# Agent attention with a gated convolution: a batch's transposed rows in one buffer of five pairs, and loads that the planner holds back

## The chip, the core and the metric

The kernel runs on one core of one Trainium2 chip. The metric is device time in microseconds (us): the median of several runs of the same program. Beside it stands one profiled execution, whose trace shows each instruction of each engine: TensorE (PE, with its weight loads as PEld), VectorE (DVE), ScalarE (ACT), GpSimd (POOL) and SyncE (SP), whose queue (SPq) issues nearly all the DMAs.

## What is computed

Four batches of 12,800 rows with 128 columns, 49 agents. Attention runs twice, from agents to keys and from queries to agents; its output goes through a causal convolution of five taps that gates a projection.

```python
def sm(a, b):                       # softmax over the last axis
    s = scale * (a @ b.transpose(0, 2, 1))
    e = np.exp(s - s.max(-1, keepdims=True))
    return e / (e.sum(-1, keepdims=True) + 1e-09)

agent_v = sm(agents, k) @ v                      # 49 x 128 per batch
x = sm(q, agents) @ agent_v                      # 12800 x 128 per batch

xp = zeros for 4 rows, then x                    # the convolution looks back
gate_pre = sum over k in 0..4 of conv_w[k] * xp[:, k:k + S, :]
out = (sigmoid(gate_pre) * (x @ w_val)) @ w_out
```

## The kernel before

**Units, pairs and chunks.** A batch is cut into ten units of 1,280 rows; two units form a pair (`SEG` = 2,560 rows), five pairs a batch. The output is made in chunks of 512 rows, five per pair, 100 in all (the last one is cut in two).

**Stages.** For each unit of keys (`k`, line 392) PE makes scores against the agents, ACT copies them, DVE takes their maximum. For each unit of values (`v`, `agent_values`, line 461) ACT takes the exponentials, DVE transposes them, PE accumulates the agents' values in `av`. `fold` (line 513) then folds agents' values, convolution weights and `w_val` of the batch into stationary matrices `stat`, so that x itself is never made: chunks work on the attention weights of the queries. For each unit of queries (`q`, line 733) PE makes scores, DVE, POOL and ACT turn them into softmax weights, and POOL and ACT write them as half-precision pieces to `pt` (lines 778 to 798): the weights, their remainders and some copies, 128 columns for each row.

**Transposed rows.** `transposes` (`t`, line 827) turns `pt` into rows along the free axis of `x1`: the first four units through PE, the other 36 by a DMA transpose that SyncE issues (line 835, `x<-pt`). `x1s` is a ring of four buffers (line 221), each with `PAD` = 16 columns ahead of one pair. `shifts` (line 866) makes `x2` from `x1`: two DMAs (line 884, `x<-x`) copy some rows five times, each time shifted by one column, for a matmul that does five taps at once. From the fifth unit on there is one such couple of DMAs per pair, once both transposes of the pair have landed.

**The preceding columns.** The convolution looks back four rows. The first four columns that a pair needs lie at the end of the pair before, in another buffer. `halo` (line 813) has POOL copy these four columns in front of the pair (line 819), or set them to zero where a batch begins (line 816).

**Chunks.** `gates` (`g`, line 898): five matmuls on `x1`, each one column further (line 922), and one on `x2` (line 926); ACT takes the tanh. `values` (`a`, line 942): two matmuls (lines 949 and 953); DVE multiplies (line 962), ACT rounds to half precision (line 968), POOL takes the remainder `hl` (line 973). `project` (`o`, line 979): three matmuls (lines 992 to 994), ACT scales (line 1006), SyncE stores each two chunks (line 1021).

**Loads.** Each unit of k, q or v is one load of 640 or 645 KB (line 369) into a ring of `NLOAD` = 11 buffers `ld`; 120 units in all. There is no load for a batch after the last, so from the last `v` on only the loads of q are left.

**What sets the order.** The order of PE's work is written out as a string (`order`, line 1088, for instance `q2.4 k3.0 g47 a47 o45`: queries of batch 2, unit 4, then keys of batch 3, unit 0, then chunk 47). For all other engines, the `Plan` (line 68) makes a schedule: every step has an engine, an estimated duration, and the steps that it needs; DMAs also have a time on the wire. `order()` (line 94) goes through the steps in time. Of those ready on an engine it takes the one with the longest path behind it (`tail`). A load is ready as soon as the last reader of its buffer is done. The result is sorted by planned start and issued in that order, so each engine's queue, SyncE's among them, is fixed beforehand; on the chip an instruction at the head of its queue waits for what it needs, and all behind it wait too. The planner's figures set only this order, not the time.

Of the kernel before, what the change touches and what calls it, by code (L numbers as in the profile page):

```python
# [10 lines left out]
F16 = mybir.dt.float16  # L11
# [6 lines left out]
P = 128  # L18
# [4 lines left out]
UNIT = 1280  # L23
NBLK = 10
GT = UNIT // G
SEG = 2 * UNIT
CH = 512
TAPS = 5
HALO = TAPS - 1
PAD = 16  # L30
# [8 lines left out]
NLOAD = 11  # L39
NT_, NH = 3, 3  # L40
NPT = 4
NX = 4
CUT = 2
NOB = 4
LEAD = 5
# [13 lines left out]
BACKLOG = 3.0  # L59
LANES = 8  # L60
LAND = 1.4

QS = 256.0
WS = 64.0
# [3 lines left out]
class Plan:  # L68
# [22 lines left out]
        self.steps.append((engine, us, fn, need, moved, key))  # L91
        self.urge.append(urge)

    def order(self):
        n = len(self.steps)
        after = [[] for _ in range(n)]
        last = None
        for i, (engine, us, fn, need, moved, key) in enumerate(self.steps):
            for j in need:
                after[j].append(i)  # L100
            if engine == "pe":
                if last is not None and last not in need:
                    after[last].append(i)
                last = i
        tail = [0.0] * n
        for i in reversed(range(n)):
            engine, us, fn, need, moved, key = self.steps[i]
            cost = us + HOP + (moved + LAND if moved else 0.0)
            if engine == "pe":
                cost = us  # L110
            tail[i] = cost + self.urge[i] + max((tail[j] for j in after[i]), default=0.0)
        engines = ("pe", "act", "dve", "pool", "dma")
        free = dict.fromkeys(engines, 0.0)
        wire = 0.0
        lanes = [0.0] * LANES
        left = [len(s[3]) for s in self.steps]
        at = [0.0] * n
        queues = {e: [] for e in engines}
        pe = [i for i, s in enumerate(self.steps) if s[0] == "pe"]
        here = 0  # L120
        for i, s in enumerate(self.steps):
            if s[0] != "pe" and not left[i]:
                queues[s[0]].append(i)
        start = [0.0] * n
        kind = None
        done = 0
        while done < n:
            best = None
            free["dma"] = max(free["dma"], wire - BACKLOG, lanes[0])
            for e in engines:  # L130
                if e == "pe":
                    if here < len(pe) and not left[pe[here]]:
                        pick, when = pe[here], max(free[e], at[pe[here]])
                    else:
                        continue
                elif queues[e]:
                    q = queues[e]
                    soon = min(max(free[e], at[i]) for i in q)
                    open_ = [i for i in q if at[i] <= soon + 0.05]
                    pick = max(open_, key=lambda i: (tail[i], -i))  # L140
                    for i in q:
                        if tail[i] > tail[pick] + 1.0 and at[i] < soon + 0.6 * self.steps[pick][1]:
                            pick = i
                    when = max(free[e], at[pick])
                else:
                    continue
                if best is None or when < best[0]:
                    best = when, e, pick
            when, e, i = best
            engine, us, fn, need, moved, key = self.steps[i]  # L150
            if e == "pe":
                here += 1
                if key != kind:
                    when += 0.12
                kind = key
            else:
                queues[e].remove(i)
            start[i] = when
            free[e] = when + us
            end = when + us + HOP  # L160
            if moved:
                wire = max(wire, when + 0.5) + moved
                end = max(wire, when + us) + LAND
                lanes = lanes[1:] + [end]
            done += 1
            for j in after[i]:
                if i in self.steps[j][3]:
                    left[j] -= 1
                    at[j] = max(at[j], end)
                    if not left[j] and self.steps[j][0] != "pe":  # L170
                        queues[self.steps[j][0]].append(j)
        self.start = start
        return sorted(range(n), key=lambda i: (start[i], i))


@with_exitstack
def tile_agent_attention_gated_conv(
# [9 lines left out]
    nc = tc.nc  # L187
# [30 lines left out]
    qsm = ring(2, [P, NBLK], F32, "qsm")  # L218
    qr = ring(2, [P, NBLK], F32, "qr")
    pts = ring(NPT, [P, NBLK, P], F16, "pt")  # L220
    x1s = ring(NX, [P, PAD + SEG], F16, "x1_")
    x2s = ring(3, [P, SEG], F16, "x2")
    ths = ring(NT_, [P, CH], F32, "th")
    hs = ring(NH, [P, CH], F32, "h")
# [41 lines left out]
        out=fold, in0=ident[:, 0:AP_], in1=ident[:, AP_:P], op=ALU.add  # L266
    )
    nc.vector.memset(tiny, 1e-9 / QS)
    nc.vector.memset(x1s[0][:, 0:PAD], 0.0)
    for t in wst_sb:  # L270
        nc.gpsimd.memset(t[:, TAPS + 1 :, :], 0.0)

# [81 lines left out]
    def load(kind, b, u):  # L354
        i = taken[0] % NLOAD
        taken[0] += 1
        slot_of[kind, b, u] = i
        if kind == "v":
            dst, src = ld[i], vP[b, u].rearrange("p n c -> p (n c)")
        else:  # L360
            dst = ld[i][:, 0:UNIT]
            src = (kT if kind == "k" else qT)[b, :, u * UNIT : (u + 1) * UNIT]
        parts = [(dst, src, [("ld", i), ("ld2", i)])]
        if (kind, b, u) == ("v", 0, NU - 1):
            h = VW // 2
            parts = [(dst[:, 0:h], src[:, 0:h], [("ld", i)]), (dst[:, h:], src[:, h:], [("ld2", i)])]
        for d, f, keys in parts:
            add(
                "dma", 0.4, lambda d=d, f=f: nc.sync.dma_start(out=d, in_=f), (), keys,
                1.57 / len(parts),  # L370
            )

    def score_matmuls(b, src, out):
# [425 lines left out]
    def on_pe(b, u):  # L799
        g = b * NU + u  # L800
        return g < PE_FIRST or (g < (B - 1) * NU and g % TURN in PE_TURNS)

    def unit_rows(g):
        o = PAD + g % 2 * UNIT
        return x1s[g // 2 % NX][:, o : o + UNIT]

    def row_keys(s, halves):


        i = s % NX  # L810
        return [(x, i, h) for h in halves for x in ("x1", "x1b")] + [("x1h", i)] * (0 in halves)

    def halo(s):
        to = x1s[s % NX][:, PAD - HALO : PAD]
        if s * 2 % NU == 0:
            fn = lambda: nc.gpsimd.memset(to, 0.0)
            read = []
        else:
            fn = lambda: nc.gpsimd.tensor_copy(
                out=to, in_=x1s[(s - 1) % NX][:, PAD + SEG - HALO : PAD + SEG]  # L820
            )
            read = [(x, (s - 1) % NX, 1) for x in ("x1", "x1b")]

        read.append(("x2", (s - 1) % 3, UNIT, 0))
        add("pool", 0.1, fn, read, [("x1h", s % NX)])

    def transposes(b, u):
        g = b * NU + u
# [37 lines left out]
    def shifts(b, u):  # L866

        g = b * NU + u
        if g >= SINGLE and g % 2 == 0:
            return  # L870
        n = 1 if g < SINGLE else 2
        u0 = u + 1 - n
        s = g // 2
        x2, x1 = x2s[s % 3], x1s[s % NX]
        o = (g + 1 - n) % 2 * UNIT
        src = row_keys(s, range(0, g % 2 + 1))
        c = PAD - HALO + o
        for r0, r1, every, us in X2CUTS:
            first = A + (2 if every == 3 else 3 * THREES)
            rows = x1[first : first + 1 + (r1 - r0 - 1) * every : every, c : c + 1]  # L880
            view = [rows.ap[0], (1, TAPS), (1, n * UNIT)]
            add(
                "dma", 0.6,
                lambda r0=r0, r1=r1, rows=rows, view=view: nc.sync.dma_start(
                    out=x2[r0 * TAPS : r1 * TAPS, o : o + n * UNIT],
                    in_=bass.AP(rows.tensor, rows.offset, view),
                ),
                src, [("x2", s % 3, o + i * UNIT, r0) for i in range(n)], us * n,
            )
        if g % 2 and (g + 1) // 2 < B * NU // 2:  # L890
            halo((g + 1) // 2)


    chunks = [(t // NCH, t % NCH * CH, CH) for t in range(NT - 1)]
# [3 lines left out]
    def gates(t):  # L898
# [10 lines left out]
        halves = sorted({(b * NU + n // UNIT) % 2 * UNIT for n in (n0, n0 + w - 1)})  # L909
        segs_ = sorted({(b * NU + n // UNIT) // 2 for n in (n0, n0 + w - 1)})  # L910
        assert len(segs_) == 1
        x2, x1 = x2s[segs_[0] % 3], x1s[segs_[0] % NX]
        o2 = n0 - (segs_[0] * SEG - b * N)
        xs = row_keys(segs_[0], halves_)
        x2k = [("x2", segs_[0] % 3, h, c[0]) for h in halves for c in X2CUTS]
# [2 lines left out]

        def matmuls():
            for k in range(TAPS):  # L920
                c = PAD - HALO + o2 + k
                nc.tensor.matmul(  # L922
                    out=pg, lhsT=stat[:, k, :], rhs=x1[:, c : c + w],
                    start=(k == 0), stop=False,
                )
# [9 lines left out]
            lambda: nc.scalar.activation(out=th, in_=pg, func=AF.Tanh, scale=unscale[:, 0:1]),  # L935
            [at_g, ("unscale", x)], [("th", t % NT_)],
        )
        return stat, x2, o2, xs, x2k, st, th

    state = {}  # L940

    def values(t):
        b, n0, w = chunks[t]
        stat, x2, o2, xs, x2k, st, th = state.pop(t)
        pv, at_v = banks[t][2:]
        scale = w / CH

        def matmuls():
            nc.tensor.matmul(  # L949
                out=pv, lhsT=stat[:, TAPS, :], rhs=x1s[(b * NCH + n0 // CH) // 5 % NX][:, PAD + o2 : PAD + o2 + w],  # L950
                start=True, stop=False,
            )
            nc.tensor.matmul(  # L953
# [184 lines left out]
            done += 1  # L1138
        run[w[0]](*w[1:])

    for i in plan.order():
        plan.steps[i][2]()


# [42 lines left out]
```

## Time and profile before

| | us |
|---|---|
| median of 3 runs | 425.89 (425.65 to 426.75) |
| span of the profiled execution | 423.6 |
| PE busy | 403.9 |
| ACT busy | 301.5 |
| DVE busy | 293.3 |
| POOL busy | 228.2 |

The rows of the profile read thus. A row of a timeline has start and length in us, engine, line of the kernel, operation, tiles written and read (buffer numbers left out), and a count where several instructions are merged; in square brackets the idle time ahead of it and what ended it. `SPq` rows are DMAs being issued: their length is how long SyncE was at it, not how long the data took. In the chain of waits, `DMA x<-pt` with a length is the stretch from issue to landing. The DMA row of the page shows the busy share of the core's sixteen DMA engines in tenths, in 40 equal slices of the span.

### The profile page before, as it was taken

The page shows a single profiled execution, that of the slowest core. Times are in us where ns is not written, and L with a number is a line of the kernel's source. Part 1 is how long each engine was busy: PE and PEld are TensorE (multiplying, and loading weights), DVE is VectorE, ACT ScalarE, POOL GpSimd, SP SyncE. Part 2 cuts the span into 40 slices and gives each one's busy share as a digit, 9 for nine tenths or more (in the row PEclk, how much of TensorE's full clock was granted, in tenths as well). Part 3 has the DMA queues.
Part 4 walks back from the last instruction along what each step waited for, and adds up shares of the span by engine and source line. Part 5 has one row for each costly group of instructions (what it writes and reads, how often), then busy time and mean ns, then how long its engine had stood idle before and what let it go on. Part 6 is the DMA issues. An engine that isn't in the chain of part 4 may idle for free.

```text
span 423.6 us, 10042 instructions
## 1 busy us (share of the span) xinstructions
PE 403.9 (95%) x3907; PEld 197.0 (47%) x3907; DVE 293.3 (69%) x562; ACT 301.5 (71%) x521; POOL 228.2 (54%) x263
## 2 busy tenths in 40 slices
PE   4979999999999999999999899999999989999995
PEld 1358434346555443446555343335555534344443
DVE  3757899867875978667795575767765678676231
ACT  1564568779966777678876486778876567788776
POOL 1002557654657565554566355574366277877553
PEclk9969999999999999999999899999999999999998
DMA  8999999999999999999999999999999977755733
GB/s 320 420 417 411 370 367 353 301 295 310 412 293 283 346 317 362 304 278 356 351 379 324 271 299 370 314 332 302 296 393 322 239 196 161 199 163 176 205 121 124
DMA packets 75129, 127.62 MB, mean 301 GB/s; under 512 B 50466, under 2 KB 50850, under 8 KB 75084
## 3 DMA queue, kind: packets, MB, share of 16 engines
q1 hardware_dynamic: 74940, 126.87, 96.9%
q8 instruction: 30, 0.49, 0.5%
q10 hardware_dynamic: 144, 0.13, 0.2%
q14 instruction: 15, 0.12, 0.1%
HBM read 79.25 MB, written 26.21 MB: 249 GB/s over the span
## 4 chain that ended last, share of the span: by engine, by line
PE 78%; DMA 9%; DVE 8%; ACT 1%; POOL 1%; issue 1%; SPq 0%; POOLq 0%; DVEq 0%; ACTq 0%
PE gate L922 23%; PE sc L376 17%; PE av L480 10%; PE val L949 5%; PE out L992 5%; PE val L953 5%; PE gate L926 5%; PE out L993 4%; DMA ld<-kT 4%; PE out L994 4%; DMA x<-pt 3%; DMA x<-x 2%; DVE h L962 1%; DVE qw L772 1%; DVE qsm L763 1%
## 5 line engine op out<-in xcount | busy, mean ns | idle before, releaser
L973 POOL TENSOR_TENSOR hl<-h,hh 128x512 f16<-128x512 f32 (+1 forms) x101 | 116.9, 1158 | 96.1 <-ACT hh L968 96.0
L922 PE MATMUL gate<-x,stat 128*128 128x512 f16 (+1 forms) x500 | 125.2, 380 | 0.2 <-ACT th L935 0.2
L962 DVE SCALAR_TENSOR_TENSOR h<-th,val 128x512 f32<-128x512 f32 x100 | 67.8, 678 | 66.8 <-PE out L993 26.2
L376 PE MATMUL sc<-ld,ag_sb 128*32 128x320 f32 x1280 | 101.5, 447 | 7.6 <-DMA ld<-kT 7.0
L935 ACT ACTIVATE th<-gate,unscale 128x512 f32<-128x512 f32 x100 | 68.3, 683 | 33.3 <-PE gate L926 31.7
L1006 ACT ACTIVATE ob<-out,oscale 128x512 f32<-128x512 f32 x98 | 67.3, 687 | 21.3 <-PE out L994 20.1
L922 PEld LDWEIGHTS <-stat 128*128 128x128 f16 x505 | 46.3, 97 | 63.7 <-issue 14.8
L968 ACT CAST hh<-h 128x512 f16<-128x512 f32 (+1 forms) x101 | 61.5, 609 | 17.2 <-DVE h L962 16.4
L750 POOL TENSOR_TENSOR qw<-sT,qmx 128x490 f32<-128x490 f32 x40 | 41.4, 1035 | 47.6 <-DVE qmx L745 47.5
L376 PEld LDWEIGHTS sc<-ld,ag_sb 128*32 128x32 f32 x1280 | 36.7, 111 | 59.4 <-issue 25.7
L480 PE MATMUL av<-ld,eT 128*32 128x129 f32 (+1 forms) x1400 | 50.7, 279 | 1.0 <-DVE eT L386 1.0
L480 PEld LDWEIGHTS av<-ld,eT 128*32 128x32 f32 (+1 forms) x1400 | 47.1, 117 | 7.5 <-issue 2.5
L794 POOL TENSOR_TENSOR pt<-qw,pt 128x490 f16<-128x490 f32 x40 | 44.8, 1120 | 3.1 <-ACT pt L779 2.9
L471 ACT ACTIVATE e<-ks,kbias 128x320 f32<-128x320 f32 x80 | 39.3, 554 | 5.4 <-DVE eT L386 3.3
L386 DVE STREAM_TRANSPOSE sT<-sc 128x640 f32<-128x640 f32 x40 | 33.6, 839 | 13.4 <-PE sc L376 12.7
L402 ACT COPY ks<-sc 128x640 f32<-128x640 f32 x40 | 27.7, 691 | 21.2 <-PE sc L376 19.1
L386 DVE STREAM_TRANSPOSE eT<-e 128x640 f32<-128x640 f32 x40 | 33.5, 842 | 9.8 <-ACT e L471 5.2
L926 PE MATMUL gate<-x,stat 95*128 95x512 f16 x100 | 38.3, 383 | 1.5 <-DMA x<-x 1.5
L949 PE MATMUL val<-x,stat 128*128 128x512 f16 x100 | 38.2, 382 | 0.8 <-DVE h L962 0.6
L953 PE MATMUL val<-x,stat 95*128 95x512 f16 x100 | 38.1, 381 | 0.0
L994 PE MATMUL out<-hl,wo 128*128 128x512 f16 x98 | 37.0, 378 | 1.1 <-POOL hl L973 1.1
L992 PE MATMUL out<-hh,wo 128*128 128x512 f16 x98 | 37.3, 381 | 0.1
(130 smaller groups left out, 389.4 us busy)
## 6 DMA issues: line engine op xcount, KB each, us to landing
ld<-kT SPq DMA_DIRECT2D x40, 640.0 KB
ld<-qT SPq DMA_DIRECT2D x40, 640.0 KB
ld<-vP SPq DMA_DIRECT2D x39, 645.0 KB
outT<-ob SPq DMA_DIRECT2D x48, 512.0 KB
x<-x SPq DMA_DIRECT2D x18, 375.0 KB
x<-x SPq DMA_DIRECT2D x18, 100.0 KB
outT<-ob SPq DMA_DIRECT2D x3, 256.0 KB
x<-x SPq DMA_DIRECT2D x4, 187.5 KB
```

Of the source, the lines that this page charges most:

```text
L376: nc.tensor.matmul(out=out[g * BLK : (g + 1) * BLK, j, 0:GT], lhsT=ag_sb[:, b, j * BLK : (j + 1) * BLK], rhs=src[:, g * GT : (g + 1) * GT] ...
L386: nc.vector.transpose(out=out.rearrange("p n (j i) -> p j n i", j=2), in_=in_.rearrange("p j (n i) -> p j n i", i=BLK),)
L480: nc.tensor.matmul(out=av[o + j : o + j + cols, 0 : C + 1], lhsT=et[:, n, j : j + cols], rhs=vt[:, n, :], start=(u == 0 and n < 2), stop=( ...
L922: nc.tensor.matmul(out=pg, lhsT=stat[:, k, :], rhs=x1[:, c : c + w], start=(k == 0), stop=False,)
L926: nc.tensor.matmul(out=pg, lhsT=stat[0 : TAPS * X2R, TAPS + 1, :], rhs=x2[0 : TAPS * X2R, o2 : o2 + w], start=False, stop=True,)
L935: lambda: nc.scalar.activation(out=th, in_=pg, func=AF.Tanh, scale=unscale[:, 0:1]),
L949: nc.tensor.matmul(out=pv, lhsT=stat[:, TAPS, :], rhs=x1s[(b * NCH + n0 // CH) // 5 % NX][:, PAD + o2 : PAD + o2 + w], start=True, stop=False,
L953: nc.tensor.matmul(out=pv, lhsT=stat[0 : TAPS * X2R, TAPS + 2, :], rhs=x2[0 : TAPS * X2R, o2 : o2 + w], start=False, stop=True,)
L962: lambda: nc.vector.scalar_tensor_tensor(out=h, in0=th, scalar=1.0, in1=pv, op0=ALU.add, op1=ALU.mult),
L968: "act", 0.16 + 0.42 * scale, lambda: nc.scalar.copy(out=hh, in_=h),
L973: lambda: nc.gpsimd.tensor_tensor(out=hl, in0=h, in1=hh, op=ALU.subtract),
L1006: lambda: nc.scalar.activation(out=ob[:, o : o + w], in_=po, func=AF.Copy, scale=oscale),
```

## The change

There are two parts.

One: `x1` is one buffer of `NX` = 5 pairs behind 16 zero columns. A pair's place is its number modulo five, so the first pair of each batch always comes behind the zero columns, and every other pair right behind the pair before. `halo` and its 19 POOL instructions are gone. `row_keys` makes a reader of a pair's first half also a reader of the second half of the pair before (in the planner's bookkeeping). Shifts and matmuls take their columns from the one buffer; their shapes stay.

Two: `late_loads` takes the place of `order` at the end. It makes the plan once as before, notes for each load the planned start of the first step that reads it, and makes the plan again with each load not ready earlier than `AHEAD` = 14 us before that start. PE's written order stays.

```diff
-NX = 4
+NX = 5
...
+AHEAD = 14.0
...
-    def order(self):
+    def order(self, held=None):
...
-        at = [0.0] * n
+        at = list(held or [0.0] * n)
...
+    def late_loads(self):
+        self.order()
+        held = [0.0] * len(self.steps)
+        for i, s in enumerate(self.steps):
+            for j in s[3]:
+                if self.steps[j][5] == "ld":
+                    t = self.start[i] - AHEAD
+                    held[j] = min(held[j], t) if held[j] else t
+        return self.order(held)
...
-    x1s = ring(NX, [P, PAD + SEG], F16, "x1_")
+    x1 = const.tile([P, PAD + NX * SEG], F16, name="x1")
...
-    nc.vector.memset(x1s[0][:, 0:PAD], 0.0)
+    nc.vector.memset(x1[:, 0:PAD], 0.0)
...
-                1.57 / len(parts),
+                1.57 / len(parts), key="ld",
...
+    def pair_at(s):
+        return PAD + s % NX * SEG
+
     def unit_rows(g):
-        o = PAD + g % 2 * UNIT
-        return x1s[g // 2 % NX][:, o : o + UNIT]
+        o = pair_at(g // 2) + g % 2 * UNIT
+        return x1[:, o : o + UNIT]
 
     def row_keys(s, halves):
-        i = s % NX
-        return [(x, i, h) for h in halves for x in ("x1", "x1b")] + [("x1h", i)] * (0 in halves)
-
-    def halo(s):
-        to = x1s[s % NX][:, PAD - HALO : PAD]
-        if s * 2 % NU == 0:
-            fn = lambda: nc.gpsimd.memset(to, 0.0)
-            read = []
-        else:
-            fn = lambda: nc.gpsimd.tensor_copy(
-                out=to, in_=x1s[(s - 1) % NX][:, PAD + SEG - HALO : PAD + SEG]
-            )
-            read = [(x, (s - 1) % NX, 1) for x in ("x1", "x1b")]
-
-        read.append(("x2", (s - 1) % 3, UNIT, 0))
-        add("pool", 0.1, fn, read, [("x1h", s % NX)])
+        keys = [(x, s % NX, h) for h in halves for x in ("x1", "x1b")]
+        if 0 in halves and s % NX:
+            keys += [(x, s % NX - 1, 1) for x in ("x1", "x1b")]
+        return keys
...
-        c = PAD - HALO + o
+        c = pair_at(s) - HALO + o
...
-        if g % 2 and (g + 1) // 2 < B * NU // 2:
-            halo((g + 1) // 2)
...
-                c = PAD - HALO + o2 + k
+                c = o1 - HALO + o2 + k
...
-    for i in plan.order():
+    for i in plan.late_loads():
         plan.steps[i][2]()
```

More of the change, by code (lines that the diff above doesn't have):

```diff
@@ L873, in shifts @@
         s = g // 2
-        x2, x1 = x2s[s % 3], x1s[s % NX]
+        x2 = x2s[s % 3]
         o = (g + 1 - n) % 2 * UNIT
         src = row_keys(s, range(0, g % 2 + 1))
-        c = PAD - HALO + o
+        c = pair_at(s) - HALO + o
         for r0, r1, every, us in X2CUTS:
@@ L911, in gates @@
         assert len(segs_) == 1
-        x2, x1 = x2s[segs_[0] % 3], x1s[segs_[0] % NX]
+        x2 = x2s[segs_[0] % 3]
+        o1 = pair_at(segs_[0])
         o2 = n0 - (segs_[0] * SEG - b * N)
@@ L937, in gates @@
         )
-        return stat, x2, o2, xs, x2k, st, th
+        return stat, x2, o1 + o2, o2, xs, x2k, st, th
     state = {}
@@ L943, in values @@
         b, n0, w = chunks[t]
-        stat, x2, o2, xs, x2k, st, th = state.pop(t)
+        stat, x2, o1, o2, xs, x2k, st, th = state.pop(t)
         pv, at_v = banks[t][2:]
@@ L949, in matmuls @@
             nc.tensor.matmul(
-                out=pv, lhsT=stat[:, TAPS, :], rhs=x1s[(b * NCH + n0 // CH) // 5 % NX][:, PAD + o2 : PAD + o2 + w],
+                out=pv, lhsT=stat[:, TAPS, :], rhs=x1[:, o1 : o1 + w],
                 start=True, stop=False,
```

## The prediction

> **What bounds the kernel now.** I read the page first, for the busiest engine and for the DMA queues.
>
> ```profile
> span 423.6 us, 10042 instructions
> PE 403.9 (95%) x3907; PEld 197.0 (47%) x3907; DVE 293.3 (69%) x562; ACT 301.5 (71%) x521; POOL 228.2 (54%) x263
> ...
> PEclk9969999999999999999999899999999999999998
> DMA  8999999999999999999999999999999977755733
> ...
> DMA packets 75129, 127.62 MB, mean 301 GB/s; under 512 B 50466, under 2 KB 50850, under 8 KB 75084
> ```
>
> TensorE (PE) is busy for 95% of the span, so a change that leaves its instructions alone can only win back its gaps and its slow clock. The DMA row shows a second resource without reserve: sixteen engines busy in every slice from 2 to 32 (10.6 us each, to about 339 us), idle only afterwards. The next view is busy time in stretches; its columns are the stretch and its length, then busy time and instructions of PE, PEld, DVE, ACT, POOL, then granted clock, DMA share and GB/s.
>
> ```profile
> 0.00:60.00 60.00, 48.10 (x573) 28.67 (x574) 41.80 (x92) 29.27 (x51) 14.33 (x29) 0.94 0.99 384
> 60.00:232.00 172.00, 171.93 (x1857) 83.83 (x1859) 132.52 (x237) 132.45 (x231) 102.87 (x113) 1.00 1.08 330
> 232.00:242.00 10.00, 8.50 (x53) 3.76 (x48) 4.69 (x16) 4.03 (x7) 3.94 (x6) 0.83 1.13 262
> 242.00:331.00 89.00, 89.00 (x945) 42.41 (x941) 63.53 (x118) 67.90 (x119) 50.22 (x55) 1.00 1.08 328
> 331.00:348.00 17.00, 15.31 (x119) 7.16 (x110) 11.05 (x32) 9.56 (x18) 8.05 (x10) 1.00 1.05 225
> 348.00:414.00 66.00, 65.84 (x355) 28.23 (x354) 38.16 (x67) 52.70 (x88) 45.32 (x49) 1.00 0.60 164
> ```
>
> Between 60 and 414 us PE is idle for 0.07 + 1.50 + 0 + 1.69 + 0.16 = 3.42 us. Two places hold nearly all of it: 232 to 242, where the clock is down too, and 331 to 348. The waits of PE in 60 to 424 us name what ended each (total, times, longest):
>
> ```profile
> PE gate L926 <- DMA x<-x: 1.5, 1, 1.5
> PE out L994 <- POOL hl L973: 1.1, 1, 1.1
> PE val L949 <- DVE h L962: 0.6, 1, 0.6
> ```
>
> No load of k, q or v stands there: after 60 us PE never waits for the transfers that the planner now delays. They can only have hurt by being in front of something else. The chain of waits up to 242 us shows this for the first gap.
>
> ```profile
> 220.73 7.50 DMA x<-pt
> 228.22 0.02 SPq L884
> 228.25 0.03 issue
> 228.28 7.34 DMA x<-x
> 235.62 0.05 issue
> 235.67 0.39 PE gate L926
> ...
> 236.89 2.24 PE gate L922 x5
> ```
>
> A transpose (x<-pt) takes 7.50 us from issue to landing, then the shift that reads it (x<-x) takes 7.34, and the matmul of line 926 starts as it lands. The five matmuls behind it take 2.24 us.
>
> **The part that moves: loads held back.** SyncE's queue before that gap, with one transpose from late in the kernel as a measure:
>
> ```profile
> 208.55 0.33 SPq L369 DMA_DIRECT2D ld<-qT  x1
> 208.97 0.45 SPq L369 DMA_DIRECT2D ld<-kT  x1
> ...
> 211.21 0.33 SPq L369 DMA_DIRECT2D ld<-kT  x1
> 212.77 7.23 SPq L835 DMA_TRANSPOSE x<-pt  x1
> 220.10 0.53 SPq L369 DMA_DIRECT2D ld<-kT  x1
> 220.73 2.63 SPq L835 DMA_TRANSPOSE x<-pt  x1
> ...
> 372.59 1.37 SPq L835 DMA_TRANSPOSE x<-pt  x1
> ```
>
> And PE's queue right behind the gap, where two of these loads are used:
>
> ```profile
> 241.20 2.36 PE L376 MATMUL sc<-ld,ag_sb 128*32 128x320 f32 x32
> 243.49 1.25 PE L922 MATMUL gate<-x,stat 128*128 128x512 f16 x5
> ```
>
> With the queues full, issuing a transpose holds SyncE for 7.23 us; when the loads are over, at 372 us, for 1.37. The q and k loads issued at 208.55 and 208.97 are q2.4 and k3.0 of the written order, first used by the 32 matmuls at 241.20: 32 us ahead (the k load at 211.21 is for later still). In the planner a ready load competes with a transpose by its tail (the longest path behind it). A slot free early therefore lets loads for 241 us go in front of a transpose whose shift is due at 235.
>
> The new plan does not let a load start more than 14 us before its consumer's planned start. At 212 us loads due after 226 are no longer eligible, so these three leave the queue ahead of the transpose. The same 120 loads are issued, each at about the 0.33 to 0.53 us of SyncE seen above; they move on SyncE past the transposes (L835), the shifts (L884) and the stores (L1021). They cost no engine time. Bytes do not change either.
>
> What this returns: from the chain, the shift landed 7.34 + 7.50 us after the transpose's issue, and PE stood still for 1.50 of that. If transpose and shift come 1.5 us sooner, the gap is gone. Only two transposes at 1.37 instead of 7.23 + 2.63 already give 7.1 us. I take the full 1.50. The clock goes with it: the stretch was granted 0.83 for 10 us, and 10 x (1 - 0.83) = 1.70 us of matmul time. The five gate matmuls show it, 2.24 us at 236.89 and 1.25 at 243.49. The row of 331 to 348, whose gaps are shorter, keeps a clock of 1.00. [...] Next in line after the gap: nothing PE waits for, by the rows of 60:232 and 242:331 (idle 0.07 and 0).
>
> The bill for holding is the cover that the loads lose. Bounds: nothing, as PE waits for no load now; below nothing is excluded for the same reason. From above, one stall of the kind just priced, 1.50 + 1.70 = 3.2, per load that comes late. I take nothing, since an early transpose also shortens SyncE's holds; the other end is a rival.
>
> **The part that goes: the copies on POOL (GpSimd).** Its groups, by line (busy, mean ns | idle before them):
>
> ```profile
> L819 POOL COPY x<-x 128x4 f16<-128x4 f16 x16 | 3.0, 187 | 16.9 <-DMA x<-pt 16.4 <-issue 0.5
> L816 POOL MEMSET x<- 128x4 f16 x3 | 0.3, 102 | 0.0
> ```
>
> 19 instructions and 3.3 us of POOL's work go, worth nothing by themselves on an engine 54% busy. The 16.4 us in which POOL stood in its queue for a transpose matter: everything behind the copy waits too. Once it reached PE:
>
> ```profile
> 338.78 0.19 POOL L819 COPY x<-x 128x4 f16<-128x4 f16 x1 [5.99 <-DMA x<-pt]
> 338.93 2.27 POOL L973 TENSOR_TENSOR hl<-h,hh 128x512 f16<-128x512 f32 x2
> ...
> 340.13 0.38 PE L994 MATMUL out<-hl,wo 128*128 128x512 f16 x1 [1.11 <-POOL hl L973]
> ...
> 341.79 0.47 DVE L607 TENSOR_SCALAR wst<-gw,rs 128x245 f16<-128x245 f32 x1 [2.08 <-POOL gw L541]
> ...
> 346.25 0.38 PE L949 MATMUL val<-x,stat 128*128 128x512 f16 x1 [0.58 <-DVE h L962]
> ```
>
> POOL waited 5.99 us for the copy, with two subtractions (hl) behind it; PE waited 1.11 for the first. The folding of the next batch's weights (gw on POOL, then DVE) came late by the same copy, and 0.58 at 346.25 is its echo. Without the copy nothing on POOL waits for a transpose. I take 1.11 in full. The 0.58 lies between 0 (DVE's queue is as full some other way) and 0.58; I take half, 0.29.
>
> **One buffer, five pairs.** A gate matmul and a shift now read the preceding pair's last four columns in place. That adds a dependence on the preceding pair's second transpose, which had landed before, as the copy needed it; queued behind it are only that chunk's own matmuls. A transpose into a place must also wait for the pair that reads across its edge: it comes five pairs later instead of four, so it waits for less. The matmuls' shapes do not change. Cost: nothing.
>
> **The sum.** Against the profiled run: 423.6 - 1.50 - 1.70 - 1.11 - 0.29 = 419.0 us of span. The median of the runs is 425.89, 2.3 above that span; I carry the 2.3 over: 421.3 us, 1.1% less. A measurement of this kernel can tell about 0.3% (1.3 us) from no change.
>
> **Rivals.** *Late loads (slower).* In the first 20 us, when only loads are queued, the chain has
>
> ```profile
> 7.55 12.53 DMA ld<-kT
> ```
>
> 12.53 us from issue to landing of one load. Behind a queue as full as that, a load issued 14 us ahead lands 1.5 us before its use, and any hold of SyncE over 1.5 us (a transpose's 2.63 or 7.23) makes it late. That is where this decides: landing time plus hold over 14. For it: the DMA row has no idle slice before 339 us, so what is deferred can't be caught up quickly. Against it: fewer loads in flight land sooner. Two stalls of 3.2 us outweigh the gain: 421.3 + 6.4 = 427.7; each further one adds 3.2. [...]
>
> *The gap stays (same).* The transpose at 220.73 may be waiting for its own rows on POOL, or loads due at 229 to 231 us, still eligible at 215, may take the place of those removed. Then 3.2 us stay and only the copy's 1.1 is won: 424.8.
>
> *One buffer serialises.* If waits were kept per buffer and not per region, each transpose would wait for all matmuls that read x1, and they for it: 36 times the 7.50 + 7.34 us of the chain above, 534 us more. Against it: in
>
> ```profile
> 13.07 0.82 DVE L411 TENSOR_REDUCE kmx<-ks 128x2 f32<-128x640 f32 x1 [0.34 <-ACT ks L402]
> ...
> 13.42 0.69 ACT L402 COPY ks<-sc 128x640 f32<-128x640 f32 x1 [0.38 <-PE sc L376]
> ```
>
> DVE reads one unit of the single buffer ks while ACT writes another.
>
> **How the numbers follow.** Forecast 0.60; late loads 0.23, as the DMA engines have no idle slice before 339 us; the gap stays 0.15; serialised 0.02. Faster by over 0.3%: 0.60; within it: 0.15; slower: 0.25. The low end is 420.0: the sum with the whole 0.58 (421.0) and 1 us of the 11.9 us that PE idles in the first 60 (60 - 48.10), should the new order fill them better. The high end is 427.7, late loads with two stalls. About 2 in 10 lie outside: half of the late loads, the serialised case, and a little below. For the forecast alone, 420.0 to 422.9 (one stall of half that price).
>
> **What would show it.** Right: no wait of PE L926 for x<-x; granted clock 1.00 from 60 to 414 us; no POOL wait for x<-pt; transposes issued in about 1.4 to 3 us in mid-kernel; loads issued some 14 us before use; DMA digits below 9 before slice 32. Wrong: waits of PE L376 or L480 for ld after 60 us with the clock down behind them (late loads); L926 still waiting (the gap stays); x<-pt waiting for PE gate (serialised).

## The result and the profile after

| | median of runs, us | against before |
|---|---|---|
| before | 426.32 (425.65 to 427.00, 4 runs) | 1 |
| after | 442.94 (441.94 to 446.38, 4 runs) | 1.0404, 95% interval 1.0373 to 1.0435 |

The change makes the kernel 4% slower. The profiled execution took 442.06 us, with a span of 440.0. In the kernel after, the lines of before are found thus: loads L382 (was L369), transposes L839 (L835), shifts L888 (L884), stores L1024 (L1021), scores L389 (L376), agents' values L493 (L480), gates L925 and L929 (L922 and L926).

The page of the kernel after, its first lines, the clock and the DMA engines:

```profile
span 440.0 us, 10019 instructions
PE 407.9 (93%) x3907; PEld 196.5 (45%) x3907; DVE 292.7 (67%) x562; ACT 301.9 (69%) x521; POOL 226.1 (51%) x244
...
PEclk9969999999999969999999998999999999999998
DMA  8999999999989999979999979999999989997633
```

PE's share fell from 95 to 93%, and its busy time rose, because the clock row now has two dips in mid-kernel (slices 15 and 25, counted from 1) where it had one. The DMA row, all 9 from slice 2 to 32 before, has digits of 7 and 8 in the middle (slices 12, 18, 24): the engines that carry the loads run short of work, although PE waits for loads. The stretches of the kernel after show where the time is (columns as in the prediction):

```profile
60.00:414.00 354.00, 337.87 (x3223) 157.51 (x3220) 244.12 (x461) 253.60 (x440) 200.14 (x206) 0.99 0.98 286
...
150.00:160.00 10.00, 4.62 (x33) 1.60 (x35) 4.03 (x11) 4.60 (x8) 2.66 (x4) 0.89 0.94 238
160.00:165.00 5.00, 5.00 (x26) 1.68 (x19) 2.32 (x4) 0.07 (x1) 2.22 (x3) 0.54 0.94 283
...
265.00:275.00 10.00, 9.53 (x69) 3.44 (x70) 4.04 (x7) 3.78 (x7) 2.39 (x4) 0.83 1.04 347
```

From 60 to 414 us PE is idle for 354 - 337.87 = 16.1 us (3.4 before). The clock takes 10 x 0.11 + 5 x 0.46 + 10 x 0.17 = 5.1 us (1.7 before). Together 12.7 + 3.4 = 16.1 us more, and the span grew by 16.4. The waits of PE in the same stretch, kernel after (total, times, longest):

```profile
PE sc L389 <- DMA ld<-kT: 7.9, 4, 4.3
PE av L493 <- DMA ld<-vP: 4.2, 4, 2.1
PE sc L389 <- DMA ld<-qT: 3.3, 4, 1.5
```

The wait of the gate for x<-x and that for POOL's hl are gone, as forecast. In their place stand twelve waits for loads, 15.4 us, where before there was none. What made the loads late shows in the waits of SyncE's queue over the whole span. Kernel after:

```profile
SPq L888 <- DMA x<-pt: 39.4, 16, 4.9
SPq L839 <- DMA x<-x: 36.5, 11, 7.0
```

And before:

```profile
SPq L884 <- DMA x<-pt: 32.7, 16, 3.8
```

That a shift waits for the transpose that it reads (x<-pt) is old. New is the second line of after: eleven times a transpose (L839) waits at the head of SyncE's queue until a shift (x<-x) has landed, for 36.5 us in all. Among SyncE's waits in the kernel before, no transpose stands waiting for a shift. One such place, in SyncE's queue of the kernel after:

```profile
121.62 1.20 SPq L382 DMA_DIRECT2D ld<-vP  x1
122.92 1.66 SPq L888 DMA_DIRECT2D x<-x  x2
131.66 1.66 SPq L839 DMA_TRANSPOSE x<-pt  x1
133.37 1.53 SPq L382 DMA_DIRECT2D ld<-kT  x3
135.00 0.60 SPq L382 DMA_DIRECT2D ld<-qT  x1
135.69 4.23 SPq L839 DMA_TRANSPOSE x<-pt  x1
139.97 1.34 SPq L1024 DMA_DIRECT2D outT<-ob  x2
141.40 3.38 SPq L839 DMA_TRANSPOSE x<-pt  x1
149.72 0.93 SPq L888 DMA_DIRECT2D x<-x  x1
150.74 0.51 SPq L382 DMA_DIRECT2D ld<-kT  x1
151.36 1.43 SPq L382 DMA_DIRECT2D ld<-qT  x1
```

SyncE issues the two DMAs of a shift at 122.92, and nothing more until 131.66. The larger of the two landed at 131.59. Everything behind that transpose comes late as well: the next transposes, the shift at 149.72 that needs them, and behind that shift the two loads at 150.74 and 151.36. On PE at the same time:

```profile
152.29 0.38 PE L956 MATMUL val<-x,stat 95*128 95x512 f16 x1
156.97 1.63 PE L389 MATMUL sc<-ld,ag_sb 128*32 128x320 f32 x16 [4.29 <-DMA ld<-kT]
159.69 2.36 PE L389 MATMUL sc<-ld,ag_sb 128*32 128x320 f32 x16 [1.09 <-DMA ld<-qT]
...
162.17 2.34 PE L925 MATMUL gate<-x,stat 128*128 128x512 f16 x5
```

The two loads are the ones that PE wants at 152.7; it stands still for 4.29 and 1.09 us, and then runs at half the clock (2.34 for five gate matmuls instead of 1.24).

Why should a transpose into one pair's columns wait for a shift that reads another pair's? The data do not overlap. In the built program 14 of the 36 transposes have a wait for the larger DMA of the shift of the pair before, which reads each third partition (15 partitions, five times each); none has such a wait for the smaller one, which reads four neighbouring ones. (SyncE's DMAs also share eight semaphores in turn, in all kernels here, so that one can come to wait for the eighth DMA before it. The kernel before has four transposes that wait for a shift in this way, and none that waits for one otherwise.) It seems that the programming layer that puts in the waits takes a read of each third partition for a read of more than it touches; how it reckons was not looked into. With a buffer per pair, as before, the two are different tensors and the question does not arise.

### The profile page after: what moved, and what is told of

Read it like the earlier page. It is cut to its first block, busy times and chain, and to the rows that moved or that the text cites. A ratio compares the mean times of both kernels' runs of the same rounds, so it can differ in the third digit from the quotient of the medians.

```text
span 440.0 us, 10019 instructions
## 1 busy us (share of the span) xinstructions
PE 407.9 (93%) x3907; PEld 196.5 (45%) x3907; DVE 292.7 (67%) x562; ACT 301.9 (69%) x521; POOL 226.1 (51%) x244
## 4 chain that ended last, share of the span: by engine, by line
PE 73%; DMA 19%; DVE 4%; ACT 1%; issue 1%; POOL 0%; SPq 0%; POOLq 0%; DVEq 0%; ACTq 0%
PE gate L925 22%; PE sc L389 15%; PE av L493 10%; DMA ld<-kT 7%; DMA ld<-vP 6%; DMA ld<-qT 5%; PE val L952 4%; PE out L995 4%; PE val L956 4%; PE gate L929 4%; PE out L996 4%; PE out L997 4%; DVE sT L399 1%; DVE qw L785 0%; ACT th L938 0%
## 5 line engine op out<-in xcount | busy, mean ns | idle before, releaser
L925 PE MATMUL gate<-x,stat 128*128 128x512 f16 (+1 forms) x500 | 126.0, 382 | 0.3 <-ACT th L938 0.2
L389 PE MATMUL sc<-ld,ag_sb 128*32 128x320 f32 x1280 | 104.3, 455 | 18.9 <-DMA ld<-kT 15.0
L925 PEld LDWEIGHTS <-stat 128*128 128x128 f16 x505 | 46.5, 98 | 64.7 <-issue 16.2
L971 ACT CAST hh<-h 128x512 f16<-128x512 f32 (+1 forms) x101 | 61.5, 609 | 17.0 <-DVE h L965 16.1
L389 PEld LDWEIGHTS sc<-ld,ag_sb 128*32 128x32 f32 x1280 | 36.6, 112 | 72.7 <-issue 26.5
L493 PE MATMUL av<-ld,eT 128*32 128x129 f32 (+1 forms) x1400 | 51.1, 279 | 5.5 <-DMA ld<-vP 4.2
L493 PEld LDWEIGHTS av<-ld,eT 128*32 128x32 f32 (+1 forms) x1400 | 46.5, 116 | 13.4 <-DVE eT L399 3.4
L424 DVE TENSOR_REDUCE kmx<-ks 128x2 f32<-128x640 f32 x39 | 31.6, 813 | 12.1 <-ACT ks L415 12.1
L929 PE MATMUL gate<-x,stat 95*128 95x512 f16 x100 | 38.2, 382 | 0.5 <-DMA x<-x 0.5
## 6 DMA issues: line engine op xcount, KB each, us to landing
x<-x SPq DMA_DIRECT2D x18, 375.0 KB, 4.3
```

The costliest lines, as they stand in the source:

```text
L389: nc.tensor.matmul(out=out[g * BLK : (g + 1) * BLK, j, 0:GT], lhsT=ag_sb[:, b, j * BLK : (j + 1) * BLK], rhs=src[:, g * GT : (g + 1) * GT] ...
L493: nc.tensor.matmul(out=av[o + j : o + j + cols, 0 : C + 1], lhsT=et[:, n, j : j + cols], rhs=vt[:, n, :], start=(u == 0 and n < 2), stop=( ...
L925: nc.tensor.matmul(out=pg, lhsT=stat[:, k, :], rhs=x1[:, c : c + w], start=(k == 0), stop=False,)
L929: nc.tensor.matmul(out=pg, lhsT=stat[0 : TAPS * X2R, TAPS + 1, :], rhs=x2[0 : TAPS * X2R, o2 : o2 + w], start=False, stop=True,)
L971: "act", 0.16 + 0.42 * scale, lambda: nc.scalar.copy(out=hh, in_=h),
```

## Experiments

Two theories stood at the start. **H**: holding the loads back makes them late by itself. **W**: the one buffer brings a wait of transposes for shifts, SyncE stands, and what is queued behind it is late. The rival of both, that the two need each other, was settled by crossing the parts. Ratios are against the kernel before on the same chip, with 95% intervals.

**First: each part alone.** Holding alone is the kernel before with this:

```
-    for i in plan.order():
+    for i in plan.late_loads():
```

(and `late_loads` with its keys). One buffer alone is the kernel after with that line turned back.

> The kernel before (four separate buffers, POOL's copies kept) with one part of the change alone: loads held back to 14 us. Theory H (holding alone makes the loads late: the planned 14 us shrink to 5 to 10 us in SyncE's queue): about 437 to 445 us, PE waiting 10 us or more for ld after 60 us. Theory W (the one buffer adds a wait of each pair's first transpose for the landing of the preceding shift, SyncE stands still for it, and only that makes the held loads late): 421 to 426 us, PE waiting under 2 us for ld.

> The changed kernel with loads as early as before: one buffer of five pairs, no copies on POOL, plan not repeated. Theory H: the one buffer is harmless, 421 to 426 us. Theory W: the transposes still wait for the shifts (some 30 us of SyncE in all), but loads have a cover of 20 to 30 us, so PE waits little for ld; shifts that are just in time come later, 426 to 432 us.

Measured: holding alone 427.75 us, 1.001 (0.9985 to 1.0035); one buffer alone 440.82, 1.0289 (1.0235 to 1.0343). The waits of PE from 60 to 414 us, first with holding alone:

```profile
PE av L493 <- DMA ld<-vP: 3.3, 2, 1.8
PE sc L389 <- DMA ld<-kT: 1.3, 1, 1.3
```

then with one buffer alone, and SyncE's wait in that kernel:

```profile
PE gate L929 <- DMA x<-x: 14.8, 5, 5.7
```

```profile
SPq L839 <- DMA x<-x: 55.8, 13, 6.6
```

Both times missed what either theory gave: holding alone lies between the two ranges, and one buffer alone is 9 us above the higher one. Holding alone gives back what it gains. The gap at 232 to 242 us and its slow clock are gone, and three late loads cost 4.6 us. So H is right that loads come late, and wrong that this explains 16 us. The 14 us are the planner's; on the chip the loads of q and k after 60 us are issued about 10 us before their first use (median; 9.6 with holding alone, 10.0 in the kernel after). One buffer alone has no late load, since they are issued some 20 us ahead (median 22); there the shifts are late instead, and PE waits 14.8 us for them. The clock then stays at half for 3.41 + 6.83 + 6.83 us behind those waits. By these two runs the larger loss is in the one buffer, and holding the loads changes which transfer PE waits for.

**Second: one buffer without the wait, a first attempt that failed.** If reading each third partition brings the wait, reading neighbouring ones should not. The rows that a shift reads were made neighbours, with the weights reordered to fit:

```
-X2CUTS = ((0, THREES, 3, 0.5), (THREES, X2R, 1, 0.3))
+X2CUTS = ((0, THREES, 1, 0.5), (THREES, X2R, 1, 0.3))
...
-            first = A + (2 if every == 3 else 3 * THREES)
+            first = A + NDUP + r0
```

> The changed kernel with the rows of x2 side by side instead of each third one (other agents take part in the doubled rows; the sums are the same), so that the 75-row shift reads neighbouring partitions and no transpose has a wait for it. Order of all queues as in the changed kernel. Theory W: 421 to 426 us, no wait of x<-pt for x<-x, PE's waits for ld mostly gone. Theory H: the waits for x<-x go, the late loads stay, 436 to 443 us.

> As the run before, with loads as early as in the kernel before: one buffer, no copies on POOL, no wait of a transpose for a shift, no holding. Both theories: 421 to 426 us; the gap at 235 us (3.2 us with its clock) may stay, the waits for POOL's copies (1.4) go, so about 424.5.

Measured: 459.86 with held loads, 1.0758 (1.0698 to 1.0818); 447.42 without, 1.0442 (1.0365 to 1.0520). The wait of transposes for shifts was gone from SyncE's queue, so it does hang on the partition step. But both kernels were slower still, far from what both theories gave. The page's line for the larger DMA of a shift points to a reason: kernel after, then the one here with held loads (count, KB, median us from issue to landing, which the page can tell for only three of the 18):

```profile
x<-x SPq DMA_DIRECT2D x18, 375.0 KB, 4.3
```

```profile
x<-x SPq DMA_DIRECT2D x18, 375.0 KB, 7.0
```

The edit changed two things at once, and these two runs alone say nothing on the wait. What the rows cost by themselves was measured on the kernel before, with the same edit and nothing else:

> The kernel before (four buffers, copies, loads not held) with the rows that a shift reads made 15 and 4 neighbouring partitions instead of each third one. It measures by itself what the earlier pair of runs with such rows mixed in. Theory W with slow shifts: shifts from neighbouring rows are slower (6 to 8 us unloaded instead of 4), and this alone costs much: 440 to 450, about what the one buffer with such rows and without the wait took (447.4). If it stays at 425 to 430, the rows cost nothing and the one buffer costs some 4% even without the wait, which speaks against W.

Measured: 449.12 us, 1.0532 (1.0485 to 1.0580). The neighbouring rows alone cost 5%. With them, four buffers take 449.1 us and one buffer without the wait takes 447.4. So one buffer without its wait is no slower than four (it also does without the copies, which the fifth experiment prices at about 1%).

**Third: five pairs in five buffers, all else as in the kernel after.** This isolates the wait without touching the shifts. The kernel leaves out the four columns ahead of a pair, which stay at zero. The instructions and their order are those of the kernel after on all engines, but for DVE, which clears five stretches of columns at the start instead of one.

```
-    x1 = const.tile([P, PAD + NX * SEG], F16, name="x1")
+    x1s = ring(NX, [P, PAD + SEG], F16, "x1_")
...
-    nc.vector.memset(x1[:, 0:PAD], 0.0)
+    for t in x1s:
+        nc.vector.memset(t[:, 0:PAD], 0.0)
```

> The kernel after, instruction for instruction in the same order on every engine, but its five pairs lie in five separate buffers, each with its own zero columns; the four columns before a pair are left at zero and not copied, so the first four outputs of a pair are computed from zeros. Only the waits that a shared buffer brings are gone. Theory W (the loss is the wait of a pair's first transpose for the shift of the pair before, which one buffer brings): the SyncE waits for x<-x vanish, the four-round load waits of TensorE fall from 15.4 us to about 4 to 5 as in the rings with held loads, and the time is 422 to 429. Rival H (holding the loads in this order, with five pairs and no copies, is itself what costs): 438 or more.

> The same, with loads in the order of the kernel without holding; it differs from the one buffer without holding only in that wait. Theory W: 421 to 427 (the time before, up to 1.4 us less for the copies' wait), against 440.8 with one buffer. Rival (five pairs, no copies and their order cost): 437 or more.

Measured: 425.49 us with held loads, 0.9967 (0.9940 to 0.9993), against 442.94 with one buffer; 421.24 without holding, 0.9882 (0.9835 to 0.9930), against 440.82. SyncE's queue of the held kernel, same place as above (transposes L837, shifts L886, loads L383):

```profile
120.95 1.69 SPq L886 DMA_DIRECT2D x<-x  x2
123.86 5.54 SPq L837 DMA_TRANSPOSE x<-pt  x1
129.45 1.52 SPq L383 DMA_DIRECT2D ld<-kT  x3
...
142.11 0.93 SPq L886 DMA_DIRECT2D x<-x  x1
143.14 0.50 SPq L383 DMA_DIRECT2D ld<-kT  x1
```

The transpose starts 1.2 us after the shift was issued, 7.6 us before it lands (131.45). The load that came at 150.74 is issued at 143.14. PE's waits for loads fall from 15.4 us to 3.0, and no clock is lost from 60 to 414 us:

```profile
PE av L494 <- DMA ld<-vP: 2.8, 3, 1.6
...
PE sc L390 <- DMA ld<-kT: 0.2, 1, 0.2
```

That is the verdict for W, twice: with the buffers apart, 17 and 20 us are gone (19 and 17 by the ratios, as the kernels compared were not timed together). The built programs say what else differs, with held loads: apart from the clears, waits of SyncE's queue alone. There the 14 waits of transposes for a shift are gone, and two waits of a shift for a transpose of the pair before, whose last columns it no longer reads. The waits of all other engines are the same. The 425.49 us of the held kernel are still 4 us more than without holding.

**Fourth: how far ahead.** `AHEAD = 22.0` instead of 14.0, in three kernels: the kernel before with holding, the kernel after, and the five buffers apart.

> The kernel before with loads held, but only to 22 us before their use instead of 14. With 14 the time was 427.75: the mid-kernel gap and its half clock went (3.2 us) and 4.6 us of late loads came. Theory: with 8 us more lead the late loads go and the gap stays closed: 422 to 425. Rival: some loads then stand ahead of a transpose again and the gap returns: 425.5 to 428.

> The kernel after with loads held to 22 us before their use instead of 14. Theory W (the shared buffer's wait makes SyncE stand up to 7 us, and what is issued next comes late): with 22 us of lead the loads survive the standing, as at the unheld order, but the shifts behind the standing stay late: waits for loads under 4 us instead of 15.4, waits for x<-x of 5 to 15 us, time 432 to 441. Rival H2 (the 14 us were too short, and the one buffer only shows it): 420 to 425, as the rings at 22 (420.5).

> The five separate buffers with zero columns left at zero and no copies, loads held to 22 us. Rings with four buffers and copies had no TensorE wait over 0.5 us left at 22 (420.5). So with TensorE the bound and nothing left to gain from copies or the fifth buffer: 418.5 to 421.5. If the copies or the fourth buffer still cost something in the rings at 22, this falls below 418.5.

| buffers | not held | held to 22 us | held to 14 us |
|---|---|---|---|
| four, with copies | 1 | 420.50, 0.9863 (0.9823 to 0.9902) | 427.75, 1.001 |
| five apart, no copies | 421.24, 0.9882 | 420.81, 0.9859 (0.9811 to 0.9908) | 425.49, 0.9967 |
| one, no copies | 440.82, 1.0289 | 429.83, 1.0054 (1.0019 to 1.0089) | 442.94, 1.0404 |

The kernel before with loads held to 22 us leaves nothing out and beats both kernels, by 1.4% and about 5%; it came out below both ranges expected for it. After 60 us its loads of q and k are issued 19.6 us before their first use (median; 14.5 to 27.5). These are all its PE waits from 60 to 414 us:

```profile
PE sc L1005 <- DVE h L975: 0.5, 1, 0.5
PE sc L1007 <- POOL hl L986: 0.4, 1, 0.4
PE gate L935 <- ACT th L948: 0.2, 1, 0.2
```

PE is idle for 1.3 us in that stretch, at full clock. Five buffers without copies are no faster, since nothing is left to win there. The one buffer at 22 us fell between what the two theories gave, and missed both: the wait is as long as ever, but costs 8 to 9 us instead of 17 to 20. Its SyncE line and its PE waits:

```profile
SPq L839 <- DMA x<-x: 52.4, 14, 6.9
```

```profile
PE gate L929 <- DMA x<-x: 3.4, 3, 2.0
PE sc L389 <- DMA ld<-kT: 1.3, 1, 1.3
PE sc L389 <- DMA ld<-qT: 1.2, 2, 0.9
PE av L493 <- DMA ld<-vP: 1.1, 2, 0.8
```

The rows fit that the standing of 52.4 us is shared out between loads and shifts, and that most of it meets some slack of each. No gap is longer than 2.0 us and no clock is lost. The sum of SyncE's standing therefore does not give the loss (36.5 and 55.8 us of it cost 17 to 20, 52.4 us cost 8 to 9); what counts is what has too little lead behind each stand.

**Fifth: the copies and the fifth place, each alone,** in the kernel before, loads not held. `NX = 5` in the one; in the other `halo` and its keys removed, and the columns of all four buffers cleared at the start. Apart from those copies and clears, every engine has the instructions of before in their order.

> The kernel before with a ring of five buffers instead of four; copies kept, loads not held, the order on every engine unchanged. The five separate buffers without copies took 421.2 against 427.4, 1.2% less. By the prediction the copies' wait is worth 1.4 us and the fifth buffer nothing: no change, 426 to 428. Rival (a fifth place frees transposes that wait for matmuls that still read the fourth): 421 to 424.

> The kernel before without the copies on GpSimd; the four columns before a pair stay zero in its four buffers, so the first four outputs of a pair are computed from zeros. Order on the other engines unchanged. By the prediction: 1.4 us less, 425 to 426.5. Rival (the copies, which hold the subtractions behind them until a transpose lands, delay the transposes as well and make the mid-kernel gap): 421 to 423, as with five.

Measured: a fifth buffer 425.42 us, 0.9952 (0.9919 to 0.9984); no copies 422.81, 0.9906 (0.9874 to 0.9938). The fifth buffer came out between what the prediction and its rival gave; without the copies the time is what the rival gave. The copies were worth 0.6 to 1.3%, 2.7 to 5.4 us, more than the 1.40 forecast. Without them PE's wait for hl is gone. The gap at 232 to 242, which the fifth buffer leaves open (2.2 us, with 3.41 us of half clock), shrinks to 0.37 us at full clock, without any load being held; the waits for x<-x that are left are short:

```profile
PE gate L911 <- DMA x<-x: 2.4, 3, 1.1
```

```profile
235.23 0.39 PE L911 MATMUL gate<-x,stat 95*128 95x512 f16 x1 [0.37 <-DMA x<-x]
```

The rival's reason is not shown by this. The shift behind that gap is issued at 227.99 instead of 228.28, hardly sooner; PE comes to the matmul 0.7 us later, and had stood for 0.9 us at 93.8 for another shift. How the copies cost more than the wait for hl stays open.

## Why the prediction was wrong

The forecast was 421.3 us in a range of 420.0 to 427.7; 442.94 lies far outside.

- **The failed step is "One buffer, five pairs ... Cost: nothing".** It followed the real dependences of the data. On the chip the waits count that are built into the program, and those included one of the next pair's transpose for a shift. In the runs that wait costs 17 to 20 us with loads not held or held to 14 us, and 8 to 9 with 22 us of lead. Of the 21.6 us between forecast and result, 17.4 go with the shared buffer (442.94 against 425.49); the other 4.2 are the next failed term.
- **"One buffer serialises"** came near, in the wrong form. It asked whether waits are kept per buffer or per region, found two engines at once in two units of `ks`, and was given 0.02. The reads of `ks` there take all 128 partitions. The shift is the one reader of x1 that steps over partitions, and no row shown spoke about such a read. Nothing serialised on PE's matmuls; a wait of 14 transposes, on the queue that issues all loads, was enough.
- **"The bill for holding: ... I take nothing"** was wrong as well. Alone, with four buffers, holding to 14 us costs 4.6 us in three late loads, which cancels its gain. It was the point where the rival of late loads decides: landing time plus hold over 14. The rows of the prediction gave more than 14 for it (12.53 + 2.63), and the sum should have taken some of it. The changed kernel in five buffers shows the size: 425.49 with 14 us, 4.2 above the forecast, and 420.81 with 22.
- **Late loads as a rival** is what the profile after shows, PE waiting at L389 and L493 for ld, with the clock down behind. But two stalls were priced, and there were twelve waits; and their cause was not the 14 us alone. That fewer loads in flight land sooner, which spoke against this rival, is so in the kernel before: by the median a load lands 5.2 us after its issue with no other load in flight, 7.8 with two and 12.5 with seven. It did not keep the loads here from being late.
- **The gap and its clock (1.50 + 1.70)** went as forecast wherever loads were held and the buffers kept apart. With four buffers the shift that ends the gap is issued at 225.46 us (14 us of lead) or 217.98 (22 us) instead of 228.28. With four buffers and 22 us the span was 417.7, against 419.0 in the sum. But the gap also shrank to 0.37 us with the copies left out and no load held, so holding is not the only way to close it. That the clock goes with every such stall was too much: the three late loads with four buffers and 14 us (gaps of 1.85, 1.27 and 1.49 us) cost no clock at all.
- **The copies (1.11 + 0.29)** were priced by the one wait that reached PE; the run without them gave 2.7 to 5.4.
- **The signs of being right** came in part although the kernel was slower: no wait of the gate for x<-x, no wait of POOL for x<-pt, DMA digits below 9 before slice 32. They show that the two forecast gains came, not what else the change brought; the loads, "issued some 14 us before use" by that list, were issued 10 us ahead.

So the gains that the prediction counted are real, but they do not add up: holding to 22 us alone gives 420.50, leaving out the copies alone 422.81, both together, in five buffers, 420.81. The change loses them, and 17 us more, for the most part through a wait that its diff does not show.

## What to carry to other kernels

Before joining buffers, list the waits that the built program has at each instruction of the fullest in-order queue, and compare them with the list before: here a read that steps over partitions brought 14 transposes a wait that the data did not need, and SyncE's queue stood still for 36.5 us, with all that was behind it. Give held transfers a lead of landing time plus the longest hold of their queue, here 8.2 us (the loads of the kernel before after 60 us, by the median) and 7.2 (the longest issue, the transpose at 212.77), so 15.4 us by estimate. The planner's 14 us, 10 on the chip, were too short, and its 22, 20 on the chip, were enough with separate buffers; nothing between was run. When an edit made to take one cost away changes a second, run it on the kernel before as well; crossing the two gave the answer that the edit alone could not.

## What the runs showed of the hardware

**Shifts from neighbouring partitions landed later.** With the loads over and one store still on its way, the larger DMA of a shift lands 4.1 us after its issue when it reads each third partition (kernel before, at 397 us), and 6.3 when it reads 15 neighbouring ones (four buffers with neighbouring rows), with the same number of rows and bytes (375.0 KB). The smaller one, which reads the same four partitions in both and is issued right behind, goes from 4.2 to 7.7 us; it stands in the chain of the four buffers with neighbouring rows:

```profile
421.99 7.68 DMA x<-x
```

So the DMA whose partitions did not change was later too. What makes them late is not shown by any run here.

**The clock and short gaps.** In the kernels before and after, behind the first 30 us, gaps of PE of 1.0 to 2.1 us were sometimes followed by half clock and sometimes not. In the kernel before, 1.50 us up to 235.67 was (3.41 us of half clock from 236.98), 1.11 us at 339.0 was not. In the kernel after, 1.96 us at 263.1 was (3.41 us from 267.0), while 2.10 us at 200.8 was not, nor were 1.18, 1.50 and 1.54 us at 256.9, 318.1 and 365.5. The one longer gap, 4.29 us at 152.7, with 1.09 us soon behind it, was followed by 6.83 us of half clock from 157.77. Half clock came in pieces of 3.41 or 6.83 us in these two traces, but for the last one, which runs up to the end of the span (from 421.3 before, from 437.7 after). What decides which gap is followed by it was not shown; the length of the gap alone does not.
